# Weight combinations as sums of blocks made by adding transfers, and every second pair of blocks in turned order

## The chip, the cores and the metric

The kernel runs on one core of one Trainium2 chip. The metric is the device time of one execution in microseconds (us). Times inside an execution are counted from the start of the profiled span.

## The reference

Linear attention feeds a gated feed-forward block. Batch 4, 4 heads of 32 dims, sequence 1088, model width 128, feed-forward width 1024 (split in two halves of 512).

```python
kv = einsum('bhsf,bhsd->bhfd', phi(k), v);  z = sum_s phi(k)          # phi: product of two 8-dim sketches
x  = einsum('bhsf,bhfd->bhsd', phi(q), kv) / (phi(q) . z + 1e-6)       # -> [4, 1088, 128]
h  = gelu(x @ w_in);  u, v = h[..., :512], h[..., 512:]
v_n = (v - mean) / sqrt(var + 1e-6) * g_ln
v_s = einsum('ts,bsd->btd', w_sg, v_n) + b_sg[None, :, None]           # the large product, 1088 x 1088
out = x + (u * v_s) @ w_out
```

## The kernel before

**The large product.** `w_sg` (transposed, called `wd` in memory) is kept on chip in two words: `w_h`, the rounded one, and `w_l`, the rest. Every product of two values is made of three matmuls: high by high (L992), low by high (L993) and high by low (L994). The contraction over 1088 positions goes in nine tiles of 128 (the ninth has 64); `whole` runs all of them for one block of 128 features (`db`) and one third of the positions (`ci`, 362 to 364 columns). The ninth tile is added by `tail` (L1003, L1004).

**Seven products instead of eight.** Batches 1 to 3 treat two feature blocks at a time (`pair`), and of the nine tiles the first eight as two halves of four, and of the three column thirds the first two. That gives a 2x2 by 2x2 block product, which is made with seven block products (`product`, four tiles each) from combinations of the `v_n` blocks, made on VectorE (tile `tmp`, then `words` splits a combination into the buffer `ar`), and combinations of the weight blocks. The last column third goes through `whole` twice.

**Weight combinations.** `combine` makes them once. It loads pieces of `wd` into `tmp` (L1040, two transfers a step, eight steps), makes four combinations on VectorE (L1045 to L1048), splits each into two words (ScalarE L1050 to L1052, VectorE L1053 to L1055), and stores three of them, called "1", "3" and "2", to `td` in HBM (L1057 to L1059). The fourth stays on chip (`t4`). Plain block "b" is saved to `td` too. `stream(n, half)` later loads combination n into the middle third of `w_h` and `w_l`, over what lies there: two transfers of 362 KB (L1064) and four of 181 KB (L1066). It is called twice in batch 0 and four times in a pair, twice in the last pair.

**Attention of the next batch** (`attention(b)`) runs beside the pairs. Key features `kp` are made tile by tile: TensorE L1083, ScalarE L1086, VectorE L335, TensorE L1091. The query sketch goes out to `dq` in HBM (L1120) and comes back spread over the partitions as `ea` and `eb` (L1130, L1127), where VectorE multiplies them (L1133).

**Order.** A planner (`Plan`) writes the order of every engine before the program runs. The times that it aims at for TensorE's side work come from the tables `SIDE`, `UNITS` and `OUTS`. An engine executes its list in order, and so does the SyncE queue (SP) that issues nearly all transfers: an instruction that waits holds up all behind it.

## Time and profile before

| | |
|---|---|
| three runs | 346.93, 350.94, 351.39 us (median 350.94) |
| profiled execution | 347.09 us, of which the span is 345.3 us |
| busy | TensorE 332.4, VectorE 271.4, ScalarE 217.7, GpSimd 23.0 us |
| transfers | 68.87 MB, mean 199 GB/s |
| combination stores to `td` | 66.7 to 138.1 us of the span |

An engine's busy time says how much of the span it worked. TensorE's matmuls overlap, so its idle time is read between the starts of neighbouring matmuls: in an undisturbed stretch one of 362 columns starts 0.165 us after the one before.

### The profile page before, as it was taken

The numbers are of one execution on the slowest core, as the hardware profiler recorded it, in microseconds if no ns is written. First come the engines' busy times: TensorE is split into PE (matmuls) and PEld (weight loads), VectorE is DVE, ScalarE is ACT, GpSimd is POOL, SyncE is SP. The second block draws the span as 40 slices with busy tenths as digits, with TensorE's granted clock in tenths as the row PEclk, the third lists the DMA queues.
The fourth block names the chain that finished last, engine by engine and source line by source line (L and its number), as shares of the span: only waits on it lengthen the run. The fifth ranks groups of instructions, "written<-read, shape, count | busy, mean of one in ns | idle before, by whom it ended". The sixth has DMA issues, their size and how long they took to land.

```text
span 345.3 us, 5940 instructions
## 1 busy us (share of the span) xinstructions
PE 332.4 (96%) x1952; PEld 311.4 (90%) x1952; DVE 271.4 (79%) x619; ACT 217.7 (63%) x517; POOL 23.0 (7%) x86
## 2 busy tenths in 40 slices
PE   8998999999999979999999999999999999999995
PEld 7876559998999869889999999999999999999994
DVE  4798999998997598979973989989647765874764
ACT  5476862464579989637659986658979644332331
POOL 0002000000000330000002400000006000000000
PEclk9999999999999999999999999999999999999998
DMA  7996033566567755899996854784509905874601
GB/s 246 392 393 219 7 104 99 151 203 192 164 189 253 211 158 151 269 276 325 265 282 196 271 153 132 210 284 152 172 19 317 348 7 173 289 272 136 210 26 62
DMA packets 56175, 68.87 MB, mean 199 GB/s; under 512 B 5008, under 2 KB 53456, under 8 KB 56144
## 3 DMA queue, kind: packets, MB, share of 16 engines
q1 hardware_dynamic: 56000, 68.40, 63.2%
q8 instruction: 15, 0.25, 0.3%
q14 instruction: 16, 0.13, 0.1%
q10 hardware_dynamic: 144, 0.09, 0.1%
HBM read 59.48 MB, written 8.99 MB: 198 GB/s over the span
## 4 chain that ended last, share of the span: by engine, by line
PE 70%; DMA 13%; DVE 11%; issue 2%; ACT 2%; SPq 1%; DVEq 0%
PE bz L992 12%; PE bz L993 11%; PE bz L994 11%; DMA eb<-dq 4%; DMA td<-tmp 3%; PE pz L792 3%; PE bs L1091 2%; PE pab L668 2%; DMA tmp<-in_w 2%; DMA w_h<-td 2%; PE bs L906 2%; PE bs L907 2%; PE bs L908 2%; PE bz L1004 2%; PE bz L1003 2%
## 5 line engine op out<-in xcount | busy, mean ns | idle before, releaser
L992 PE MATMUL bz<-w_h,ar 128*128 128x362 f32 (+1 forms) x288 | 95.6, 332 | 1.9 <-DMA w_h<-td 1.3
L993 PE MATMUL bz<-w_h,ar 128*128 128x362 f32 (+1 forms) x288 | 94.7, 329 | 0.2 <-DVE ar L968 0.2
L994 PE MATMUL bz<-w_l,ar 128*128 128x362 f32 (+1 forms) x288 | 94.7, 329 | 0.0
L992 PEld LDWEIGHTS bz<-w_h,ar 128*128 128x128 f32 x288 | 54.3, 188 | 3.7 <-DMA w_h<-td 1.7
L993 PEld LDWEIGHTS bz<-w_h,ar 128*128 128x128 f32 x288 | 54.2, 188 | 1.0 <-DVE ar L968 0.5
L994 PEld LDWEIGHTS bz<-w_l,ar 128*128 128x128 f32 x288 | 54.2, 188 | 0.0
L967 ACT CAST ar<-vn 128x512 fp32r<-128x512 f32 x40 | 24.7, 620 | 23.1 <-PE bz L994 21.9
L936 ACT CAST gh<-gt 128x362 fp32r<-128x362 f32 (+1 forms) x47 | 23.1, 496 | 21.7 <-DVE gt L935 10.9
L968 DVE TENSOR_TENSOR ar<-vn,ar 128x512 fp32r<-128x512 f32 x40 | 27.3, 684 | 8.0 <-ACT ar L967 7.8
L912 ACT ACTIVATE u<-bs 128x362 f32<-128x362 f32 (+1 forms) x48 | 22.4, 470 | 15.4 <-PE bs L908 7.6
L937 DVE TENSOR_TENSOR gl<-gt,gh 128x362 fp32r<-128x362 f32 (+1 forms) x47 | 24.6, 532 | 6.7 <-ACT gh L936 6.6
L407 ACT ACTIVATE vn<-vn,st 128x512 f32<-128x512 f32 x36 | 27.7, 815 | 2.9 <-POOL st L538 2.3
L935 DVE TENSOR_TENSOR gt<-gt,u 128x362 f32<-128x362 f32 (+1 forms) x47 | 24.5, 529 | 1.5 <-ACT u L912 1.1
L922 DVE SCALAR_TENSOR_TENSOR gt<-bz,g_col,b_bc 128x362 f32<-128x362 f32 (+1 forms) x31 | 18.0, 588 | 6.4 <-PE bz L1004 4.1
L1188 ACT ACTIVATE kp<-vn,st 128x512 bf16<-128x512 f32 x27 | 19.5, 721 | 0.2
L1091 PE MATMUL bs<-vx,kp 128*128 128x128 f32 x108 | 16.4, 276 | 1.7 <-DVE kp L335 1.7
L792 PE MATMUL pz<-w_f,vn 128*128 128x362 f32 (+3 forms) x54 | 17.6, 472 | 0.3 <-ACT vn L407 0.3
L1185 ACT ACTIVATE vn<-bs 128x512 f32<-128x512 f32 x27 | 15.9, 590 | 1.7 <-PE bs L1178 1.7
L946 PE MATMUL po<-gl,wout_h 128*128 128x362 f32 (+1 forms) x47 | 15.7, 334 | 0.9 <-DVE gl L937 0.8
L1091 PEld LDWEIGHTS bs<-vx,kp 128*128 128x128 f32 x108 | 14.6, 191 | 2.0 <-DVE kp L335 2.0
L906 PE MATMUL bs<-x_h,win_h 128*128 128x362 f32 (+1 forms) x48 | 16.4, 341 | 0.0
L907 PE MATMUL bs<-x_h,win_l 128*128 128x362 f32 (+1 forms) x48 | 15.7, 328 | 0.0
(273 smaller groups left out, 744.7 us busy)
## 6 DMA issues: line engine op xcount, KB each, us to landing
w_l<-td SPq DMA_DIRECT2D x96, 181.0 KB, 5.0
w_h<-td SPq DMA_DIRECT2D x48, 362.0 KB, 4.4
w_f<-in_w SPq DMA_DIRECT2D x9, 544.0 KB, 11.2
tmp<-in_w SPq DMA_DIRECT2D x16, 181.0 KB, 2.8
vx<-in_v SPq DMA_DIRECT2D x8, 288.0 KB
ea<-dq SPq DMA_DIRECT2D x12, 182.0 KB, 3.1
eb<-dq SPq DMA_DIRECT2D x12, 182.0 KB
td<-tmp SPq DMA_DIRECT2D x8, 271.5 KB, 3.7
```

Of the source, the lines that this page charges most:

```text
L407: A.activation(self.vn(t), self.vn(t), AF.Identity, bias=self.nm[:, t : t + 1], scale=self.rs[:, t : t + 1])
L792: return mm(zs[ci], lhsT=vn[r, t, :P], rhs=w_f[t][r, c0 : c0 + cw], start=(t == 0), stop=(t == NT - 1),)
L906: mm(o, lhsT=win_h[:, ws], rhs=xh[:, cs], start=True, stop=False)
L935: add("V", dv(cw), lambda: V.tensor_mul(gt(k)[:, :cw], gt(k)[:, :cw], utt[plan.got[u]][:, :cw]), r=[u], w=[k], free=[u])
L936: add("A", ac(cw), lambda: A.copy(ght[plan.got[h]][:, :cw], gt(k)[:, :cw]), r=[k], take={h: "gh"})
L937: add("V", dv(cw), lambda: V.tensor_sub(glt[plan.got[l]][:, :cw], gt(k)[:, :cw], f32(ght[plan.got[h]][:, :cw])), r=[h, k], take={l: "gl"}, ...
L967: add("A", ac(n), lambda: A.copy(dst[:, 0], q()), r=r, w=[key])
L968: add("V", dv(n), lambda: V.tensor_sub(dst[:, 1], q(), f32(dst[:, 0])), r=r, w=[key])
L992: mm(o, lhsT=ar[e][:, 0, t], rhs=wh, start=first, stop=False, skip_group_check=True)
L993: mm(o, lhsT=ar[e][:, 1, t], rhs=wh, start=False, stop=False, skip_group_check=True)
L994: mm(o, lhsT=ar[e][:, 0, t], rhs=wl, start=False, stop=last, skip_group_check=True)
L1091: mm(ps(pkv)[:, P * p : P * p + P], lhsT=kpt[t % 3][:, P * p : P * p + P], rhs=vx[:, NT : NT + t + 2 : t + 1] if p else vx[:, t : NT + 1 : ...
```

## The change

The combinations become plain sums of blocks, so that they can be made outside the engines. `sums` copies a block of `wd` (or a finished sum) to a new HBM tensor `ud` (SyncE) and then lets GpSimd issue a transfer that adds a second block onto it. `combine` then only loads a sum, splits it into two words and stores them, through two buffers of `tmp` in turn. The signs that this moves go to the `v_n` combinations and to the gates (`g_col`, `ng_col`). Every first pair of a batch runs its seven products in turned order (`back`), so that it begins with the weight blocks that the pair before ended with. `stream` is now called once in batch 0 and twice in each pair. All tables of the planner are new, and `tmp` grows by one eighth, `rs` shrinks by a quarter.

```diff
-        k=[-69.5, -129.7, -258.62, 75.49, -16.81, -86.04, 99.22, -240.4, 467.74],
+        k=[-5.4506e+25, -1.86798e+26, -3.68831e+26, 1.20378e+26, -7.9147e+25, -9.67116e+25, 1.96766e+26, -2.06105e+26, 6.74955e+26],
...
-    rs = const([P, 4, P], "rs", F32R)
+    rs = const([P, 3, P], "rs", F32R)
-    tmp = const([P, 7 * HW], "tmp")
+    tmp = const([P, 8 * HW], "tmp")
...
+    ud = {n: dram.tile([P, 4, K2], F32, name=f"ud{n}") for n in "1324"}
+    def sums():
+        part = lambda i, j: wd[:, 4 * i : 4 * i + 4, K2 * j : K2 * j + K2]
+        for n, first, more in (("1", part(0, 0), part(0, 1)), ("2", "1", part(1, 1)), ("3", part(0, 1), part(1, 1)), ("4", "2", part(1, 0))):
+            u = isinstance(first, str)
+            load_("", 741, lambda n=n, f=first, u=u: load(ud[n], ud[f] if u else f), r=[("ud", first)] * u, w=[("ud", n)])
+            add("G", 1.2, lambda n=n, m=more: G.dma_start(ud[n], m, accum_op=ALU.add), w=[("ud", n)], late=7.0)
     def combine():
...
-                add("V", d, lambda s=s: V.tensor_sub(s[:, 0], s[:, 1], s[:, 0]), w=[k[0]], r=[k[1]])
-                add("V", d, lambda s=s: V.tensor_sub(s[:, 1], s[:, 3], s[:, 1]), w=[k[1]], r=[k[3]])
-                add("V", d, lambda s=s: V.tensor_sub(s[:, 3], s[:, 0], s[:, 3]), w=[k[3]], r=[k[0]])
-                add("V", d, lambda s=s, tl=tl: V.scalar_tensor_tensor(s[:, 2], s[:, 3], -1.0, s[:, 2], op0=ALU.mult, op1=ALU.subtract),
...
+        for i, (n, t) in enumerate((n, t) for n in "1234" for t in range(4)):
+            x, h = (tmp[:, 2 * K2 * (i % 2) + K2 * k :][:, :K2] for k in range(2))
+            load_("", 186, lambda n=n, t=t, x=x: load(x, ud[n][:, t]), r=[("ud", n)], w=[xk])
+            if n == "4":
+                add("A", ac(K2), lambda x=x, t=t: A.copy(t4(t)[0], x), r=[xk], w=[("t4", t)], after=[done_lo])
+                add("V", dv(K2), lambda x=x, t=t: V.tensor_sub(t4(t)[1], x, f32(t4(t)[0])), r=[xk], w=[("t4", t)])
+                continue
+            add("A", ac(K2), lambda x=x, h=h: A.copy(h, x), r=[xk], w=[hk])
+            add("V", dv(K2), lambda x=x, h=h: V.tensor_sub(f32r(x), x, f32(h)), r=[hk], w=[xk])
+            load_("td", 186, lambda n=n, t=t, h=h: load(TD[n][t, 0], f32(h)), r=[hk], w=[("td", n, t, 0)])
+            load_("td", 186, lambda n=n, t=t, x=x: load(TD[n][t, 1], x), r=[xk], w=[("td", n, t, 1)])
...
-    def pair(b, p, e, zi):
+    def pair(b, p, e, zi, back):
...
+        if back:
+            product(Z, zk, e[0], (0, 1), True, (1, 1))
+            stream("2", 0)
...
+            product(X, xk, e[1], (0, 0), True)
+            product(Z, zk, e[2], (4, 1), False, (1, 2))
+            stream("3", 4)
+            product(X, xk, e[3], (0, 1), False)
+            whole(Z, zk, 2, (e[1], e[0]), 0)
+            product(X, xk, e[2], (4, 1), False)
+            product(Z, zk, e[0], (4, 0), True, (0, 0))
+            product(X, xk, e[3], "t4", False, (0, 1))
+            whole(Z, zk, 2, (e[1], e[3]), 1)
+            return e[2], e[0], e[1], e[3]
...
         product(Z, zk, e[0], (0, 1), True, (1, 1))
-        if more:
-            stream("2", 0)
...
-        if more:
-            stream("3", 4)
...
+    sums()
...
         if ci == 1:
-            stream("2", 0)
-            stream("3", 4)
+            stream("1", 0)
...
-        pair(b, 0, e, zi)
+        e = pair(b, 0, e, zi, True)
...
-        pair(b, 1, e, 1 - zi)
+        e = pair(b, 1, e, 1 - zi, False)
```

On the SyncE queue, at the end of the loads of the head (the last `w_in` load is the first row), before the change `qld`, `vn` and `vx` (query, keys and values of batch 1) stand, and then the first pieces of `wd` for `combine`:

```order
L687 DMA win_raw_161<-in_w_in 128x512
L1108 DMA qld<-in_q 128x364
L1074 DMA vn<-in_k 128x9x128
L1073 DMA vx<-in_v 128x576 x2
L1040 DMA tmp<-in_w 128x2x181 x2
L1029 DMA td<-w_h 128x4x362
L1108 DMA qld<-in_q 128x364
```

And there now (`ud_610` is the sum "1", `ud_611` "3", `ud_612` "2"):

```order
L687 DMA win_raw_161<-in_w_in 128x512
L1034 DMA ud_610<-in_w 512x1x362
L1102 DMA qld<-in_q 128x364
L1068 DMA vn<-in_k 128x9x128
L1067 DMA vx<-in_v 128x576 x2
L1034 DMA ud_611<-in_w 512x1x362
L1038 DMA td<-w_h 128x4x362
L1044 DMA tmp<-ud_610 128x362 x2
L1102 DMA qld<-in_q 128x364
L1034 DMA ud_612<-ud_610 16x11584
```

One copy of a block moved ahead of the loads of batch 1, one behind them, and the loads of `tmp` now stand behind the store of `w_h` and wait for the first adding transfer.

On TensorE, at the end of the product of batch 0 over `w_f` (the weights as loaded), before the change the last four tiles run in one piece, and the first sketch of the keys of batch 1 follows:

```order
L792 MATMUL pz0_0_2_435<-w_f4_235,vn_91 128x364
L792 MATMUL pz0_0_0_431<-w_f5_243,vn_91 128x362
L792 MATMUL pz0_0_1_433<-w_f5_243,vn_91 128x362
```

Now six matmuls of later work stand between the fifth tile and the sixth:

```order
L792 MATMUL pz0_0_2_435<-w_f4_235,vn_91 128x364
L1077 MATMUL bs0_601<-sk_76,vn_91 128x128
L1108 MATMUL bs1_602<-qth_116,sk_h_78 128x364
L1109 MATMUL bs1_602<-qth_116,sk_l_79 128x364
L1110 MATMUL bs1_602<-qtl_117,sk_h_78 128x364
L1077 MATMUL bs2_603<-sk_76,vn_91 128x128
L1398 MATMUL bz0_604<-w_h_80,ar0_92 128x362
L792 MATMUL pz0_0_0_431<-w_f5_243,vn_91 128x362
```

Also on TensorE, at the key features of batch 2 (`kp`, and L1083 before, L1077 after, their sketch), before the change they follow each other with one small group between them:

```order
L946 MATMUL po0_2_890<-gl1_600,wout_h_86 128x364
L1091 MATMUL bs0_601<-vx_74,kp0_108 128x128 x2
L1083 MATMUL bs1_602<-sk_76,vn_91 128x128
L1091 MATMUL bs0_601<-vx_74,kp1_109 128x128 x2
L906 MATMUL bs2_603<-x0_h_153,win_h_84 128x364
L907 MATMUL bs2_603<-x0_h_153,win_l_85 128x364
L908 MATMUL bs2_603<-x0_l_154,win_h_84 128x364
L1091 MATMUL bs0_601<-vx_74,kp2_110 128x128 x2
L1083 MATMUL bs1_602<-sk_76,vn_91 128x128
L1091 MATMUL bs0_601<-vx_74,kp0_108 128x128 x2
```

Now the same features stand between the matmuls of a whole product:

```order
L994 MATMUL bz0_604<-w_l4_705,ar1_93 128x362
L1085 MATMUL bs0_601<-vx_74,kp2_110 128x128 x2
L1077 MATMUL bs2_603<-sk_76,vn_91 128x128
L1085 MATMUL bs0_601<-vx_74,kp0_108 128x128 x2
L992 MATMUL bz0_604<-w_h_80,ar1_93 128x362
L993 MATMUL bz0_604<-w_h_80,ar1_93 128x362
L994 MATMUL bz0_604<-w_l5_740,ar1_93 128x362
L1085 MATMUL bs0_601<-vx_74,kp1_109 128x128 x2
L906 MATMUL bs1_602<-x1_h_586,win_h_84 128x362
```

Large matmuls that TensorE did elsewhere now stand between the features, so that more time passes from one to the next.

More of the change, by code (lines that the diff above doesn't have):

```diff
@@ L1210, in pair @@
         a = {(i, j): area(b, 2 * p + i, j) for i in range(2) for j in range(3)}
         ak = {(i, j): vkeys(s, j, i) for i in range(2) for j in range(3)}
-        X, Z = (lambda: pzt[zi]), (lambda: pzt[1 - zi])
-        xk, zk = ("psn", zi), ("psn", 1 - zi)
+        banks = [(lambda: pzt[zi]), (lambda: pzt[1 - zi])]
+        bk = [("psn", zi), ("psn", 1 - zi)]
         c11, c12, c21, c22, ca, cb = (A1, 0), (A1, 1), (A2, 0), (A2, 1), (A1, 2), (A2, 2)
         end = b == B - 1 and p == 1
-        more = not end
@@ L1218, in both @@
-        def both(i, src, r):
-            add("A", ac(256), lambda: A.copy(rs[:, i : i + 2], src), r=r, w=[("rs", i), ("rs", i + 1)])
-            add("V", dv(256), lambda: V.tensor_sub(rs[64:, i : i + 2], src[64:], f32(rs[64:, i : i + 2])), r=r, w=[("rs", i), ("rs", i + 1)])
+        tk = [("tmp", i, k) for i in range(2) for k in range(2)]
+        def both(i, src, r, n):
+            w = [("rs", i + k) for k in range(n)]
+            add("A", ac(n * P), lambda: A.copy(rs[:, i : i + n], src), r=r, w=w)
+            add("V", dv(n * P), lambda: V.tensor_sub(rs[64:, i : i + n], src[64:], f32(rs[64:, i : i + n])), r=r, w=w)
@@ new lines, in rests, with total @@
+        def rests():
+            both(0, vn[:, 8, 256 * s : 256 * s + 256].rearrange("p (t d) -> p t d", d=P), ak[0, 2] + ak[1, 2], 2)
+            total(raw[:, 0], a[0, 2], a[1, 2], ak[0, 2] + ak[1, 2], ["raw"] + tk, V.tensor_sub, P)
+            both(2, raw, ["raw"], 1)
+        def total(out, x, y, r, w, f=V.tensor_add, n=512):
+            add("V", dv(n), lambda: f(out, x, y), r=r, w=w)
+        if back:
+            Z, X = banks
+            zk, xk = bk
+            total(sg, a[1, 0], a[1, 1], ak[1, 0] + ak[1, 1], ["sg"] + tk, V.tensor_sub)
+            words(ar[e[0]], lambda: sg, ("ar", e[0]), ["sg"])
+            split(b, A1, 0, e[1])
+            rests()
+            total(sg, sg, a[0, 0], ak[0, 0], ["sg"], V.tensor_sub)
+            total(s4, sg, a[0, 1], ["sg"] + ak[0, 1], ["s4"] + tk)
+            words(ar[e[2]], lambda: s4, ("ar", e[2]), ["s4"])
+            words(ar[e[3]], lambda: sg, ("ar", e[3]), ["sg"])
+            total(a[0, 0], a[0, 0], a[1, 0], ak[1, 0], ak[0, 0], V.tensor_sub)
+            product(Z, zk, e[0], (0, 1), True, (1, 1))
+            stream("2", 0)
+            split(b, A1, 1, e[0])
+            evac(b, c22, Z, zk, g_col)
+            unit(b, c12)
+            product(X, xk, e[1], (0, 0), True)
+            evac(b, c11, X, xk, g_col)
+            product(Z, zk, e[2], (4, 1), False, (1, 2))
+            stream("3", 4)
+            words(ar[e[2]], lambda: a[0, 0], ("ar", e[2]), ak[0, 0])
+            evac(b, c12, Z, zk, g_col)
+            unit(b, ca)
+            product(X, xk, e[3], (0, 1), False)
+            split(b, A2, 1, e[3])
+            evac(b, c12, X, xk, ng_col, ("gt", b, c12), False)
+            gate(b, c12)
+            unit(b, c22)
+            whole(Z, zk, 2, (e[1], e[0]), 0)
+            split(b, A2, 0, e[1])
+            evac(b, ca, Z, zk, g_col)
+            gate(b, ca)
+            unit(b, c11)
+            product(X, xk, e[2], (4, 1), False)
+            evac(b, c22, X, xk, ng_col, ("gt", b, c22), False)
+            gate(b, c22)
+            unit(b, c21)
+            product(Z, zk, e[0], (4, 0), True, (0, 0))
+            evac(b, c11, Z, zk, g_col, ("gt", b, c11), False)
+            gate(b, c11)
+            unit(b, cb)
+            product(X, xk, e[3], "t4", False, (0, 1))
+            evac(b, c21, X, xk, g_col)
+            gate(b, c21)
+            whole(Z, zk, 2, (e[1], e[3]), 1)
+            evac(b, cb, Z, zk, g_col)
+            gate(b, cb)
+            return e[2], e[0], e[1], e[3]
@@ L1222, in pair @@
+        X, Z = banks
+        xk, zk = bk
         split(b, A1, 0, e[0])
         split(b, A1, 1, e[1])
[L1224 to L1227 removed]
+        rests()
+        total(a[0, 0], a[0, 0], a[1, 0], ak[1, 0], ak[0, 0], V.tensor_sub)
@@ L1231, in pair @@
-        add("V", dv(P), lambda: V.tensor_scalar(raw[:, 0], a[1, 2], -1.0, None, op0=ALU.mult), r=ak[1, 2], w=rk)
-        add("V", dv(P), lambda: V.tensor_sub(raw[:, 1], raw[:, 0], a[0, 2]), r=ak[0, 2], w=rk)
-        both(2, raw, rk)
+        total(a[0, 1], a[0, 1], sg, ["sg"], ak[0, 1])
+        total(sg, a[1, 0], a[1, 1], ak[1, 0] + ak[1, 1], ["sg"], V.tensor_sub)
         unit(b, ca)
```

147 lines of the change are left out of this document (61 added, 86 removed).

## The prediction

> **What bounds the kernel now.** I read the page's first parts, then the engines' busy time by stretch, then TensorE's own order of time where it falls short.
>
> ```profile
> span 345.3 us, 5940 instructions
> PE 332.4 (96%) x1952; PEld 311.4 (90%) x1952; DVE 271.4 (79%) x619; ACT 217.7 (63%) x517; POOL 23.0 (7%) x86
> ...
> PE 70%; DMA 13%; DVE 11%; issue 2%; ACT 2%; SPq 1%; DVEq 0%
> ...
> 60.00:80.00 20.00, 20.00 (x128) 19.88 (x127) 17.89 (x36) 11.54 (x28) 1.01 (x1) 1.00 0.63 188
> 80.00:100.00 20.00, 19.17 (x111) 18.08 (x110) 18.90 (x46) 10.90 (x25) 0.00 (x0) 1.00 0.59 169
> 120.00:140.00 20.00, 17.29 (x115) 16.18 (x113) 18.10 (x47) 17.33 (x42) 3.21 (x11) 1.00 0.58 174
> 140.00:160.00 20.00, 18.55 (x108) 17.78 (x109) 17.02 (x36) 10.55 (x25) 0.00 (x0) 1.00 0.95 282
> 160.00:180.00 20.00, 20.00 (x120) 19.59 (x119) 17.03 (x33) 13.35 (x30) 0.00 (x0) 1.00 0.97 280
> 240.00:340.00 100.00, 100.00 (x594) 98.88 (x592) 66.41 (x132) 52.65 (x121) 6.37 (x22) 1.00 0.53 172
> ```
>
> The columns of the stretches are its length, then TensorE, weight loads, VectorE, ScalarE, GpSimd, the granted clock (1.00 throughout), the DMA share and GB/s. TensorE is busy in all of the last 100 us but for the tail, so nothing can be won there except by fewer matmuls. The DMA queues are at 0.95 to 0.97 from 140 to 180 us, and in the second half of that TensorE still loses nothing. TensorE falls short in 80 to 100 and 120 to 160 us, and there VectorE is at 17 to 19 of 20 us. So the question is which of a few stalls go. These are their rows (start, duration, what waited, and in brackets the idle time and what ended it):
>
> ```profile
> 43.40 7.78 PE L792 MATMUL pz<-w_f,vn 128*128 128x362 f32 x24 [0.31 <-ACT vn L407]
> ...
> 80.94 0.33 PE L945 MATMUL po<-gh,wout_l 128*128 128x362 f32 x1
> 81.64 0.43 PE L946 MATMUL po<-gl,wout_h 128*128 128x362 f32 x1 [0.37 <-DVE gl L937]
> 82.40 0.43 PE L992 MATMUL bz<-w_h,ar 128*128 128x362 f32 x1 [0.33 <-DVE gt L922]
> ...
> 120.19 0.32 PE L946 MATMUL po<-gl,wout_h 128*128 128x364 f32 x1
> 122.23 0.71 PE L1091 MATMUL bs<-vx,kp 128*128 128x128 f32 x4 [1.72 <-DVE kp L335]
> ...
> 125.22 0.49 PE L1083 MATMUL bs<-sk,vn 128*128 128x128 f32 x2
> 126.38 0.49 PE L1083 MATMUL bs<-sk,vn 128*128 128x128 f32 x2 [0.68 <-DVE kp L335]
> ...
> 139.94 0.43 PE L992 MATMUL bz<-w_h,ar 128*128 128x362 f32 x1 [0.29 <-DVE gt L922]
> ...
> 154.53 0.40 PE L1178 MATMUL bs<-win_l,x_h 128*128 128x512 f32 x1
> 156.19 0.43 PE L992 MATMUL bz<-w_h,ar 128*128 128x362 f32 x1 [1.26 <-DMA w_h<-td]
> ...
> 227.62 0.44 PE L946 MATMUL po<-gl,wout_h 128*128 128x362 f32 x1 [0.41 <-DVE gl L937]
> ```
>
> Each costs its bracket plus what the pipeline overlaps, which is start to start less the regular step of 0.17 us (0.23 for 512 columns): 0.70 - 0.17 and 0.76 - 0.17 at 81 and 82 us make 1.1; 2.04 - 0.17 = 1.9 at 120; 1.16 - 0.33 = 0.8 at 125; 1.66 - 0.23 = 1.4 at 154. For the other three I add 0.17 to the bracket: 0.5 at 43, 0.5 at 140, 0.6 at 227. The sum is **6.8 us**, and this is the ceiling of any gain: 2% of 347 us. Behind VectorE's lateness stand transfers:
>
> ```profile
> 80.22 0.92 DVE L1133 TENSOR_TENSOR ea<-ea,eb 128x728 f32<-128x728 f32 x1 [1.32 <-DMA eb<-dq]
> ...
> 120.93 0.92 DVE L1133 TENSOR_TENSOR ea<-ea,eb 128x728 f32<-128x728 f32 x1 [1.84 <-DMA eb<-dq]
> ...
> 141.45 0.69 DVE L1226 TENSOR_TENSOR tmp<-vn 128x512 f32<-128x512 f32 x1 [0.72 <-DMA td<-tmp]
> ...
> 225.76 0.91 DVE L1133 TENSOR_TENSOR ea<-ea,eb 128x720 f32<-128x720 f32 x1 [1.23 <-DMA w_l<-td]
> ```
>
> **The matmuls.** Both programs issue the same number of each kind (312 groups of the three large ones, 42 tails). So this term is zero, and the change can only move the stalls.
>
> **Fewer streams.** A stream is two transfers of 362 KB and four of 181 KB. The program before has 48 and 96 of them, as the rows say; the order of the new one has 26 and 52, so 13 streams for 24.
>
> ```profile
> w_l<-td SPq DMA_DIRECT2D x96, 181.0 KB, 5.0
> w_h<-td SPq DMA_DIRECT2D x48, 362.0 KB, 4.4
> ...
> tmp<-in_w SPq DMA_DIRECT2D x16, 181.0 KB, 2.8
> ```
>
> That takes out 11 x 1.45 = 16 MB of 68.9; the sums add four copies and four additions of 0.74 MB, some 6 to 9 MB. Where DMA is not waited for, this is worth nothing: at 160 to 180 us it is hidden by TensorE. What it is worth lies at 154 us. There the weights of the second product were issued as late as 148.94 and took 7.20 us in a full queue:
>
> ```profile
> 137.53 3.89 DMA td<-tmp
> ...
> 148.94 7.20 DMA w_h<-td
> ```
>
> They were late because the last store of a combination was issued at 137.5 and two streams could only then be finished. In the new program the one stream that the first pair begins with is of the sum "1", whose four stores are the first of twelve. I take the whole stall of **1.4 us** out; late next there is VectorE, whose lateness the row of 139.94 shows just before; I charge that below.
>
> **The combination on VectorE.** Seven lines of eight instructions go, 0.34 us each but for one of 0.52: these two rows stand for them.
>
> ```profile
> L1053 DVE TENSOR_TENSOR tmp<-tmp 128x362 fp32r<-128x362 f32 x8 | 4.2, 523 | 0.0
> ...
> L1045 DVE TENSOR_TENSOR tmp<-tmp 128x181 f32<-128x181 f32 x8 | 2.8, 345 | 1.5 <-DMA tmp<-in_w 1.5
> ```
>
> So 4.2 + 6 x 2.75 = 20.7 us before, and 16 of the first kind after, 16 x 0.523 = 8.4 us. 12 us less of VectorE in the stretch up to 138 us, in which it had little room. It counts only where VectorE's lateness reaches TensorE. At 120 us VectorE had itself waited 1.84 us on `eb`, so work taken away does not end that wait, but it does shorten the six features behind it; these now also stand among large matmuls, which gives each more time. I take half of 1.9 + 0.8: **1.4**. At 81 us likewise half of 1.1, **0.5**, since the same wait on `eb` stays in the program. At 140 us VectorE waited for a store out of `tmp`; the last users of `tmp` are now the four on-chip splits, which store nothing: **0.3** of 0.5. At 227 us less traffic, **0.3** of 0.6.
>
> **The six matmuls moved up.** They stand where TensorE idled at 43 us and wait for `vn`, `qld` and their casts. The last of those loads was out at 25.9 us (first row below); one copy of 0.74 MB is ahead of them now, and at the 280 GB/s of the full queue at 140 to 180 us that puts them 2.6 us later, still long before 42 us. I take **0.4** of 0.5.
>
> **The sums.** Nothing in the trace adds in HBM, so I bound it. GpSimd is free for it at 32.9 us, where its last small operation ends, and DMA then idles:
>
> ```profile
> 22.06 3.84 SPq L1073 DMA_DIRECT2D vx<-in_v  x2
> ...
> 42.09 0.37 SPq L1029 DMA_DIRECT2D td<-w_h  x1
> ...
> 32.74 0.20 POOL L538 TENSOR_TENSOR st<-np,st 128x3 f32<-128x3 f32 x1
> ...
> 30.00:40.00 10.00, 9.23 (x44) 6.53 (x43) 8.54 (x20) 6.47 (x13) 2.18 (x11) 1.00 0.15 48
> 40.00:50.00 10.00, 9.69 (x32) 5.58 (x31) 9.14 (x28) 8.54 (x17) 0.00 (x0) 1.00 0.30 94
> ...
> 52.50 0.18 ACT L1086 COPY kb<-bs 128x32 f32<-128x32 f32 x1
> ```
>
> The deadline is 52.5 us: the cast of the first sum stands behind that copy of `kb` on ScalarE, and behind it queue the next `kb` copies, on which TensorE's features wait at once. The load of the sum (2.8 us, row above) must be issued by 49.5; SyncE reaches it after the store of `w_h`, which went out at 42.1. So the first addition has from 33 to 49 us, **16 us**. Below: it costs what a plain transfer of its size does, two of 362 KB, 8.8 us, or less, since much of 4.4 us is latency. Above: two reads and a write, with the second addition beside it on the same engines, 4 x 8.8 = 35 us, and then TensorE loses 35 - 16 = 19 us. I take 9 us, the row it is nearest to, and so **nothing** for it on the path, hidden behind the preparation of the weights from 33 to 49 us. A gain below nothing is excluded: no one waits for it before.
>
> On what an addition costs, the Trainium skill, Collectives: The Full Stack, section "The bandwidth ceiling: the fold count and why AG ≠ RS ≠ AR", says that the adding step needs two source reads for each write and runs at half the rate of a copy. No trace of this kernel shows it yet; by it the addition is an estimated 17.6 us by the two 362 KB rows, 1.6 us over the deadline, and the sum would be 1.6 us smaller.
>
> **The sum.** 1.4 + 1.4 + 0.5 + 0.3 + 0.3 + 0.4 = 4.3 us. Against it, a new order on every engine brings waits of its own; the present one has seven, so I charge two of the small ones, 0.5 each. That leaves **-3.3 us**: 347.1 for the profiled execution becomes 343.8. The three runs shown lie at 346.9 and at 351 (median 350.94), where the same gain gives 347.6. I predict the middle of the two, **345.5 us**; the forecast's own range is 342 to 349.
>
> **The rivals.**
> *Nothing comes of it (20%).* For: `eb` comes by the same chain of SyncE steps, VectorE's 1.84 us stand before the features, and twelve casts of sums now stand in VectorE's and ScalarE's lists where each can hold up the rest. Against: the DMA-bound stall at 154 us has lost its cause. Time: 347.1 to 350.9, so 349.
> *All stalls go (15%).* For: all seven end in a transfer or in VectorE, and both get lighter. 347.1 - 6.8 = 340.3, or 344.1 by the median; 342.
> *The first addition comes late (12%), slower.* Mechanism: SyncE holds at the load of the first sum, then ScalarE at its cast, then TensorE at the key features. It decides from 49 us on, microsecond for microsecond. At 22 us for an addition (between the bounds of 8.8 and 35) it costs 6 and eats the gain; from there to 35 us it gives 350 to 363 us. For: SyncE's list is in order, and the query load for the next third stands behind it too. Against: 16 us of room and an idle DMA. The Trainium skill, SBUF — State Buffer, section "Who interferes with whom", says that VectorE in its two-port modes blocks GpSimd completely, the writing of its descriptors for transfers too, which would hold the addition back. The trace has a row on it:
>
> ```profile
> 68.89 1.01 POOL L805 MEMSET w_l<- 64x1088 f32 x1 [35.95 <-DVE w_l L806]
> ```
>
> GpSimd wrote 1088 columns in 1.01 us while VectorE was busy beside it with one subtraction of 1.28 us, so not every VectorE operation holds it up. VectorE's 8.5 of 10 us between 30 and 40 us are the most that could be lost, and that alone stays inside 16 us.
> *The change does not do what it says* has no room: the streams are counted in the order.
>
> **How the numbers follow.** Forecast 53%, rivals 20, 15 and 12%. Two per cent, 7 us, is about what a measurement of this kernel can tell from no change. Faster by more needs nearly the whole ceiling: the second rival and a little of the forecast, 0.16. Slower by more is most of the third, 0.09. Within 2%: 0.75. The range of 338 to 354 holds the forecast and the first two rivals with their scatter, and the mild half of the third.
>
> **What would show it.** Right: no wait on `w_h<-td` at the first pair of batch 1, 13 streams, DMA share well under 0.95 from 140 to 180 us, TensorE at 18.5 of 20 us or more from 120 to 140, and the first load of a sum issued right behind the store of `w_h`. Wrong: an idle SyncE before that load, ScalarE waiting at L1050, or TensorE waits of a kind not in the list above. I am wrong on size if the wait of VectorE on `eb` goes or doubles.

## The result, and the profile after

The changed kernel takes 359.23 us (median of 4 runs, 356.97 to 360.87), the one before 349.39 us (median of 4 as well). The ratio is 1.0316, with a 95% interval of 1.0264 to 1.0368: it is **slower by 3.2%**. The forecast was 345.5 us in a range of 338 to 354. The profiled execution took 360.87 us, with a span of 359.1 us, 13.8 us longer than before. Ratios, here and below, are taken over the fast runs alone, while the medians of the table further down count every run (one of e11 took 548 us, one of e13 843).

The first lines of the page, the engines' shares of the chain of waits, and the issues of the streams:

```profile
span 359.1 us, 5751 instructions
PE 338.1 (94%) x1952; PEld 316.2 (88%) x1952; DVE 260.0 (72%) x573; ACT 214.1 (60%) x509; POOL 28.4 (8%) x90
...
PE 58%; DMA 16%; ACT 10%; DVE 8%; SPq 2%; issue 2%; POOL 1%; POOLq 0%; DVEq 0%; ACTq 0%
...
w_l<-td SPq DMA_DIRECT2D x52, 181.0 KB
w_h<-td SPq DMA_DIRECT2D x26, 362.0 KB
```

There are as many matmuls as before (x1952), VectorE has 11.4 us less to do (271.4 before), and 13 streams are left of 24. All this came as planned. But TensorE's part of the chain fell from 70% to 58%. The stretches say where (columns as in the prediction; the seventh number is the granted clock, the eighth the DMA share):

```profile
60.00:80.00 20.00, 16.97 (x101) 16.58 (x100) 14.36 (x25) 8.03 (x21) 2.20 (x2) 0.91 0.92 248
80.00:100.00 20.00, 12.65 (x61) 12.21 (x60) 11.03 (x23) 6.41 (x14) 0.00 (x0) 0.76 0.70 163
120.00:140.00 20.00, 17.97 (x108) 17.14 (x107) 9.58 (x24) 16.11 (x45) 5.04 (x22) 0.91 0.60 176
140.00:160.00 20.00, 19.85 (x121) 19.14 (x120) 17.82 (x35) 12.95 (x29) 0.00 (x0) 1.00 0.73 223
160.00:180.00 20.00, 20.00 (x123) 19.99 (x122) 19.71 (x43) 12.13 (x25) 0.00 (x0) 1.00 0.33 105
```

From 140 to 180 us the relief is there: the DMA share is 0.73 and 0.33, where it was 0.95 and 0.97, and TensorE is short of 0.15 us where it was short of 1.45. The loss lies ahead of that, from 60 to 100 us, where TensorE lost nothing and 0.8 us before and loses 3.0 and 7.4 us now. TensorE's own order of time has the three stalls:

```profile
68.56 0.60 PE L1396 MATMUL bz<-w_l,ar 128*128 128x362 f32 x2 [3.03 <-DVE w_l L806]
...
94.51 0.67 PE L906 MATMUL bs<-x_h,win_h 128*128 128x362 f32 x1 [7.35 <-ACT u L912]
...
133.71 0.71 PE L1085 MATMUL bs<-vx,kp 128*128 128x128 f32 x4 [2.03 <-DVE kp L335]
```

and VectorE's, just ahead of each, has one instruction that waits for the same transfer each time:

```profile
66.38 0.92 DVE L1127 TENSOR_TENSOR ea<-ea,eb 128x728 f32<-128x728 f32 x1 [4.20 <-DMA eb<-dq]
...
92.16 0.92 DVE L1127 TENSOR_TENSOR ea<-ea,eb 128x728 f32<-128x728 f32 x1 [8.35 <-DMA eb<-dq]
...
132.41 0.92 DVE L1127 TENSOR_TENSOR ea<-ea,eb 128x728 f32<-128x728 f32 x1 [2.61 <-DMA eb<-dq]
```

VectorE works in order, so the low words of the weights (first stall) and the key features (third) stand behind that multiplication. In the second stall TensorE waits for `u`, and ScalarE's order of time shows that `eb` was not the only late transfer there:

```profile
89.08 0.49 ACT L1103 CAST qth<-qld 128x364 fp32r<-128x364 f32 x1 [8.21 <-DMA qld<-in_q]
...
92.89 0.49 ACT L1050 CAST tmp<-tmp 128x362 fp32r<-128x362 f32 x1 [2.39 <-DMA tmp<-ud]
93.29 0.79 ACT L1128 CAST r<-ea 128x728 fp32r<-128x728 f32 x1
93.99 0.46 ACT L912 ACTIVATE u<-bs 128x364 f32<-128x364 f32 x1
```

ScalarE waited for the query load, then for the load of a finished sum, which landed at 92.9 us, later than `eb` at 92.2; `u` stands behind that cast and behind the cast of the product `ea` (L1128), which could have begun at 93.1. So, by these rows, `eb` alone on time would have shortened this stall little. The list of waits puts the waits on `eb` at 20.2 us, against 5.5 before. Beside `eb` on the DMA engines, at 57 to 66 and at 82 to 92 us, are the third and fourth additions to go out (of sums 2 and 4; the order is 1, 3, 2, 4). GpSimd's order of time has their issues, and the view of their line the time until they landed:

```profile
33.16 1.48 POOL L1035 DMA_DIRECT2D ud<-in_w  x1
44.45 1.21 POOL L1035 DMA_DIRECT2D ud<-in_w  x1 [9.66 <-issue]
56.76 1.16 POOL L1035 DMA_DIRECT2D ud<-in_w  x1 [11.11 <-issue]
77.23 1.19 POOL L1035 DMA_DIRECT2D ud<-in_w  x1 [5.96 <-DMA ud<-ud]
```

```profile
DMA to landing us min/median/max: 10.8/11.5/13.6
```

The DMA part of the page, taken for 59.5 to 66 us and for 80 to 85 us, shows how the additions (q0, GpSimd's queue) and everything that SyncE issues (q1) share the 16 engines. The columns are packets, MB, and the time of the packets as a share of the engines' time:

```profile
q0 software_dynamic: 508, 0.72, 75.7%
q1 hardware_dynamic: 449, 0.60, 29.9%
...
q0 software_dynamic: 412, 0.59, 89.4%
q1 hardware_dynamic: 169, 0.23, 19.1%
```

The engines are full (the two shares overlap and come to over 100%), and SyncE's queue gets 30% and 19% of them: 0.60 MB in 6.5 us is 92 KB a microsecond, 0.23 MB in 5 us is 46. Before, from 160 to 180 us, the same queue moved 280. So `eb`, 364 KB that SyncE had issued by 58.4 us, landed at 66.4, and the one that it issued from 81.9 on at 92.2. The third stall is another matter: it has no addition beside it, as the fourth had landed by 90.8 us, and the kernel before had 1.72 us in that place.

A second loss rides on the stalls. Behind each of them the granted clock is low (stretches behind the first and the second):

```profile
70.00:74.00 4.00, 4.00 (x17) 4.00 (x17) 3.23 (x6) 2.03 (x5) 1.01 (x1) 0.60 0.98 270
...
94.00:102.00 8.00, 7.49 (x29) 7.50 (x30) 6.58 (x15) 4.80 (x13) 0.00 (x0) 0.59 0.53 164
```

TensorE is busy there, but at 0.60 and 0.59 of its clock, which loses 0.40 x 4.0 + 0.41 x 7.5 = 4.7 us of work. Before, the clock was 1.00 in every stretch shown. The page's first lines split the 13.8 us: TensorE idles 21.0 us where it idled 12.9, which is 8.1 more, and the same matmuls keep it busy for 338.1 us instead of 332.4, which is 5.7 more. The three stalls, 12.4 us against 6.8 in all seven before, are most of the first part. The slow clock behind the first two stalls is most of the second, and more of it lies behind the third (0.91 from 120 to 140 us).

### The profile page after: what moved, and what is told of

Read it like the earlier page. It is cut to its first block, busy times and chain, and to the rows that moved or that the text cites. A ratio compares the mean times of both kernels' runs of the same rounds, so it can differ in the third digit from the quotient of the medians.

```text
span 359.1 us, 5751 instructions
## 1 busy us (share of the span) xinstructions
PE 338.1 (94%) x1952; PEld 316.2 (88%) x1952; DVE 260.0 (72%) x573; ACT 214.1 (60%) x509; POOL 28.4 (8%) x90
## 3 DMA queue, kind: packets, MB, share of 16 engines
q0 software_dynamic: 2112, 2.97, 6.2%
## 4 chain that ended last, share of the span: by engine, by line
PE 58%; DMA 16%; ACT 10%; DVE 8%; SPq 2%; issue 2%; POOL 1%; POOLq 0%; DVEq 0%; ACTq 0%
PE bz L992 10%; PE bz L994 10%; PE bz L993 10%; DMA eb<-dq 8%; DMA tmp<-ud 3%; DMA td<-tmp 3%; PE pz L792 3%; ACT vn L407 2%; PE pab L668 2%; ACT kp L1182 2%; DMA dq<-ab 2%; PE bs L1085 2%; ACT vn L1179 2%; PE bs L906 2%; PE bs L908 1%
## 5 line engine op out<-in xcount | busy, mean ns | idle before, releaser
L992 PE MATMUL bz<-w_h,ar 128*128 128x362 f32 (+1 forms) x288 | 97.3, 338 | 0.7 <-ACT ar L967 0.3
L993 PE MATMUL bz<-w_h,ar 128*128 128x362 f32 (+1 forms) x288 | 95.4, 331 | 0.0
L992 PEld LDWEIGHTS bz<-w_h,ar 128*128 128x128 f32 x288 | 55.0, 191 | 2.9 <-DVE gt L922 1.7
L993 PEld LDWEIGHTS bz<-w_h,ar 128*128 128x128 f32 x288 | 55.0, 191 | 0.5
L994 PEld LDWEIGHTS bz<-w_l,ar 128*128 128x128 f32 x288 | 55.0, 191 | 0.0
L912 ACT ACTIVATE u<-bs 128x362 f32<-128x362 f32 (+1 forms) x48 | 22.6, 472 | 20.1 <-PE bs L908 13.6
L967 ACT CAST ar<-vn 128x512 fp32r<-128x512 f32 x37 | 22.8, 618 | 16.9 <-PE bz L994 15.9
L922 DVE SCALAR_TENSOR_TENSOR gt<-bz,g_col,b_bc 128x362 f32<-128x362 f32 (+1 forms) x37 | 21.9, 592 | 10.3 <-PE bz L1004 8.0
L968 DVE TENSOR_TENSOR ar<-vn,ar 128x512 fp32r<-128x512 f32 x37 | 25.3, 686 | 5.6 <-ACT ar L967 5.4
L906 PE MATMUL bs<-x_h,win_h 128*128 128x362 f32 (+1 forms) x48 | 17.0, 355 | 7.4 <-ACT u L912 7.4
L1127 DVE TENSOR_TENSOR ea<-ea,eb 128x728 f32<-128x728 f32 (+1 forms) x9 | 8.2, 914 | 20.2 <-DMA eb<-dq 20.2
L906 PEld LDWEIGHTS bs<-x_h,win_h 128*128 128x128 f32 x48 | 9.4, 196 | 8.2 <-ACT u L912 7.7
```

The lines of the kernel that those rows point to most:

```text
L906: mm(o, lhsT=win_h[:, ws], rhs=xh[:, cs], start=True, stop=False)
L968: add("V", dv(n), lambda: V.tensor_sub(dst[:, 1], q(), f32(dst[:, 0])), r=r, w=[key])
L992: mm(o, lhsT=ar[e][:, 0, t], rhs=wh, start=first, stop=False, skip_group_check=True)
L993: mm(o, lhsT=ar[e][:, 1, t], rhs=wh, start=False, stop=False, skip_group_check=True)
L994: mm(o, lhsT=ar[e][:, 0, t], rhs=wl, start=False, stop=last, skip_group_check=True)
```

## The experiments

**Theory A** was that the additions occupy the DMA engines, slow what is moved beside them, `eb` above all, and that TensorE's stalls follow from there through VectorE's list. **Rival B** was that the new order of the lists makes things late, whatever is moved. Unless told otherwise a kernel keeps every instruction in its place.

| run | us | ratio to before (95%) |
|---|---|---|
| changed kernel | 359.23 | 1.0316 (1.0264 to 1.0368) |
| e1: additions of 16 bytes a row | 350.02 | 1.0005 (0.9966 to 1.0044) |
| e2: copies in place of additions | 354.51 | 1.0164 (1.0114 to 1.0215) |
| e3: before, and the sums beside it | 372.89 | 1.0691 (1.0635 to 1.0747) |
| e4: turned order, sums on VectorE | 357.52 | 1.0223 (1.0151 to 1.0296) |
| e5: second and fourth addition small | 349.56 | 1.0011 (0.9964 to 1.0058) |
| e6: additions and copies small | 347.87 | 0.9987 (0.9949 to 1.0026) |
| e7: turned order, sums on GpSimd | 367.13 | 1.0526 (1.0457 to 1.0595) |
| e8: additions planned with 13 us | 360.41 | 1.0325 (1.0258 to 1.0392) |
| e9: second addition small | 356.02 | 1.0187 (1.0109 to 1.0266) |
| e10: fourth addition small | 353.77 | 1.0142 (1.0081 to 1.0203) |
| e11: sums 3 and 4 on VectorE | 349.21 | 1.0009 (0.9977 to 1.0041) |
| e12: e3 with small additions | 357.87 | 1.0202 (1.0115 to 1.0289) |
| e13: e6, `ea` and `eb` not from `dq` | 347.46 | 0.9939 (0.9897 to 0.9981) |
| e14: before, the same | 349.66 | 0.9982 (0.9934 to 1.0030) |
| e15: e13, two loads behind `eb` | 348.49 | 0.9974 (0.9932 to 1.0016) |
| e16: e6, two loads behind `eb` | 352.66 | 1.0051 (1.0011 to 1.0091) |
| e17: third addition small | 355.99 | 1.0210 (1.0107 to 1.0314) |
| e18: third and fourth addition small | 350.79 | 1.0024 (0.9981 to 1.0067) |

Prices are differences of ratios, times 349.5 us; by the intervals of the two ratios each is uncertain by 2 to 4 us. The additions are counted in the order in which they go out.

### What the additions cost

```diff
-            add("G", 1.2, lambda n=n, m=more: G.dma_start(ud[n], m, accum_op=ALU.add), w=[("ud", n)], late=7.0)
+            add("G", 1.2, lambda n=n, m=more: G.dma_start(ud[n][:, :, :4], m[:, :, :4], accum_op=ALU.add), w=[("ud", n)], late=7.0)
```

> The changed kernel with every instruction in its place, but each addition moves 16 bytes of every row instead of 1448 (the sums then lack most of their second block). Theory A (the additions occupy the DMA engines and slow whatever is moved beside them; from there eb is late, VectorE's list holds, TensorE stalls): the waits of VectorE on eb fall from 20 us to under 8, the stalls of 3.2 us at 65 and 7.5 us at 87 go, and the time falls from 359 to 344 to 349. Rival B (the new order of the lists makes eb late, whatever is moved): the stalls at 65 and 87 stay, 355 to 360.

The time is that of before, 1 us above theory A's range and far below rival B's, so the bytes of the four additions are all of the loss: 1.0316 - 1.0005 is 10.9 us, give or take 2.3. VectorE waits 8.8 us for `eb`. SyncE's queue had the engines nearly to itself while `eb` was on its way, at 57 to 60 us and at 76 to 82:

```profile
q1 hardware_dynamic: 412, 0.55, 58.9%
...
q1 hardware_dynamic: 720, 0.94, 78.2%
```

That is 183 and 157 KB a microsecond where it had been 92 and 46. The stall at 65 us is gone. Of that at 87 us 2.3 us are left, ahead of 85.4 us, which the bytes of the additions don't explain. Theory A holds, rival B doesn't.

In e2 the four transfers move the same bytes without adding.

```diff
-G.dma_start(ud[n], m, accum_op=ALU.add)
+G.dma_start(ud[n], m)
```

> The changed kernel, but the four GpSimd transfers copy the second block over the first instead of adding it (same bytes, rows and issues; the sums then lack their first block). Theory A1 (it is the adding: 135 ns for a row of 1448 bytes where a copied one takes 62): a transfer lands in 5 to 7 us instead of 11.5, most of the stalls at 65 and 87 go, 345 to 350. Rival A2 (any 0.74 MB on GpSimd's queue in that stretch does it): it lands in 9 us or more, 354 to 360. Rival B (the order alone): 355 to 360 though it lands early.

By its numbers rival A2 has it, at the lower edge: 354.5 us, and 9.7 us to landing at the median (7.3 to 10.4). But the time is half way, so half of the loss (5.6 us) is there for a plain copy too, and the other half (5.3 us) comes with the adding. The pages show what each costs the DMA engines. The first two lines are of the changed kernel, the third of this one:

```profile
q1 hardware_dynamic: 39680, 55.05, 48.9%
q0 software_dynamic: 2112, 2.97, 6.2%
```

```profile
q0 software_dynamic: 768, 2.97, 4.1%
```

6.2% of 16 x 359.1 us over 2112 packets is 169 ns for 1406 bytes, 120 ns a KB. The copy within HBM takes 4.1% of 16 x 352.6 us over 768 packets, 301 ns for 3867 bytes, 78 ns a KB. SyncE's ordinary transfers take 71 ns for 1387 bytes, 51 ns a KB. My 62 ns for a copied row was the price of SyncE's ordinary transfers, the wrong kind of copy. Adding costs 1.5 times a copy within HBM, and 2.4 times what the transfers beside it cost. The copy also went in longer packets (2 or 3 rows to one), so this run doesn't tell the adding from the shorter packets that come with it.

The next five take the additions apart: some of them move 16 bytes of a row, the others all. The first edit stands for all, with other names of sums in its list.

```diff
-G.dma_start(ud[n], m, accum_op=ALU.add)
+G.dma_start(*((x if n in "12" else x[:, :, :4]) for x in (ud[n], m)), accum_op=ALU.add)
```

> The changed kernel, every instruction in its place, with the third and fourth additions (sums 3 and 4) moving 16 bytes of a row and the first two whole (sums 3 and 4 then lack most of a block). Theory A (an addition costs by what it lies beside: the third went out at 56.8 us with eb of the first third, the fourth at 77.2 with eb of the second): both large stalls go, 350 to 352. Rival D (the first two delay the whole list: the second could only go out at 44.5, and everything behind stands 6 to 7 us later from 80 us on): 355 to 359.

> The changed kernel, every instruction in its place, only the third addition (issued at 56.8 us there) with 16 bytes of a row (sum 3 then lacks most of a block). Theory A, with shares by the stalls of the changed kernel: the stall of 3.2 us at 65 us and the slow clock behind it go (4 to 5 us), and what stands behind comes earlier; the one at 87 us stays at 4 to 8 us: 353 to 357. Rival: the fourth follows the third in every list, so all of it goes, 349 to 351.

> The same with only the fourth addition small (issued at 77.2 us). Theory A: the stall at 65 us stays at 3 us, that at 87 us shrinks from 7.5 to about the 2.5 us that it has with all additions small: 352 to 356. Rival: the late list behind the third addition alone makes the stall at 87, 357 to 360.

The first two of these expectations took sum 3 for the third to go out, and it is the second: e5 has the second and fourth small, e9 the second. So their numbers don't bear on the theories as written, and two more runs were made.

> The expectations of e5, e9 and e10 named the additions by their sums; the order in which they go out is sums 1, 3, 2, 4. So e5 had the second and fourth out small, e9 the second, e10 the fourth, and the third out was whole in all three. Here only the third out (sum 2, at 56.8 us in the changed kernel) is small, the second whole. Theory A (an addition costs by the transfers that lie beside it): nothing lies beside the first eb at 57 to 66 us, so the stall of 3.2 us at 65 us is under 1, the fourth still costs its 6 us: 354 to 357. Rival G (the second is the one that costs, since the load of sum 1 and what stands behind it lie beside it): the stall at 65 us stays over 2 us, 358 to 361.

> The changed kernel with the last two that go out (sums 2 and 4) small and the first two (sums 1 and 3) whole: what e5 was meant to be. Theory A: all of the loss goes, 348 to 351. Rival G (the second to go out costs what e9 saved, 4.5 us): 353 to 356.

e18 is even with the kernel before: the first two additions, whole, cost nothing that can be measured, and the last two all of it, 10.2 us. The third alone costs 3.7 us (e17), the fourth 6.1 (e10), together 9.8. By its time alone e17's price, 3.7 give or take 4.0 us, is not clear of nothing; what shows it is that the stall of 3.03 us is gone. Theory A holds, rival G falls. The stalls agree. TensorE's and VectorE's waits of e17, with the third out of the way, and of e10, with the fourth:

```profile
DVE ea L1127 <- DMA eb<-dq: 13.5, 5, 8.0
...
PE bs L906 <- ACT u L912: 6.8, 1, 6.8
```

```profile
DVE ea L1127 <- DMA eb<-dq: 13.6, 7, 6.1
...
PE bz L1396 <- DVE w_l L806: 5.0, 1, 5.0
```

In each the stall of the other addition stays; in e10 it is 5.0 us instead of 3.0. And e9 is no contradiction. The second addition costs 4.5 us there though it lies beside nothing that waits, since it decides when the third goes out (GpSimd's order of time in e9):

```profile
46.19 1.21 POOL L1035 DMA_DIRECT2D ud<-in_w  x1 [10.67 <-issue]
54.31 1.16 POOL L1035 DMA_DIRECT2D ud<-in_w  x1 [6.91 <-DMA ud<-ud]
```

With a small second one the third, whole, goes out at 54.31 us instead of 56.76, and the stall at 65 us is 1.19 us instead of 3.03. As e9 still has the 6.1 us of the fourth, little of its 6.4 us over e1 is left for the third: the same 0.74 MB cost some 4 us or next to nothing by 2.5 us of place, as far as these intervals tell.

e8 changes one number of the planner, so its lists differ.

```diff
-w=[("ud", n)], late=7.0)
+w=[("ud", n)], late=13.0)
```

> The changed kernel with one number of the planner changed: an addition is taken to land 13 us after its issue instead of 7 (it took 10.8 to 13.6). So casts and loads of the sums stand later in every list. Theory A (other transfers are slowed, eb above all): eb is still late, 353 to 360. Rival C (the lists wait in order on sums that were planned for too early): 345 to 350.

360.4 us: lists that give the additions 13 us gain nothing, and rival C falls. Theory A's range is missed by 0.4 us only, but its wait was wrong. The third and fourth addition went out at 63.6 and 90.5 us, `eb` was waited for 6.8 us in all, and ScalarE waited for the load of a finished sum:

```profile
79.17 0.49 ACT L1050 CAST tmp<-tmp 128x362 fp32r<-128x362 f32 x1 [4.45 <-DMA tmp<-ud]
...
104.95 0.49 ACT L1050 CAST tmp<-tmp 128x362 fp32r<-128x362 f32 x1 [4.14 <-DMA tmp<-ud]
```

TensorE stalled 4.2 us at 76 us and 3.5 at 103. Whatever transfer lies beside or behind the addition and is next in a list pays for it.

e3 puts the copies and additions into the kernel before, with nobody reading the sums; e12 is the same with additions of 16 bytes.

```diff
+    sums()
     unit(0, (1, 0))
```

> The kernel before with the four copies and four additions of the new one put into its program; nobody reads the sums, so the streams, the pairs and the combination on VectorE are those of before. Theory A: the additions slow the transfers beside them here too, VectorE's waits on eb grow from 5.5 us to over 12, and the time rises by 5 to 14 us, to 355 to 363. Rival B (the order of the new lists): no one waits for the sums, so 348 to 351.

> Control for the kernel before with the sums (372.9): the same lists, with additions of 16 bytes of a row. Theory A: additions are nearly all of the 23 us, 348 to 353. Rival B (the four copies, or the lists that were planned anew around them): 360 or more.

The additions alone raise the time by 4.9%, 17 us, without any turned order: more than I expected, as all four ran beside the key features there (52.7 to 97 us; TensorE stalled 8.2 and 6.3 us on `kp`). But e12 is at neither number: 7 us, give or take 3, are left for four copies of 0.74 MB and the lists planned around them. So e3 is not clean as a price, though it shows theory A's mechanism in another program.

e6 makes the copies small too, and loads plain blocks.

```diff
-load(ud[n], ud[f] if u else f)
+load(ud[n][:, :, :4], (ud[f] if u else f)[:, :, :4])
...
-load(x, ud[n][:, t])
+load(x, wd[:, t, :K2])
```

> The changed kernel's lists with nothing of weight moved within HBM: copies and additions move 16 bytes of a row, and the loads of the sums read a plain block of the weights in their place (the sums are then plain blocks). It prices the four copies, against the run with small additions at 350.0. Theory A (the 2.3 us packets of 46 KB of the second and fourth copy, and two more copies in the full queue before 33 us, cost something beside eb too): 346 to 349, the stall of 2.5 us at 83 smaller. Rival B (that stall comes from the order): 350, with the stall at 83 still there.

347.9 us. The copies are worth 0.2% against e1, within the intervals. The stall at 83 us fell from 2.33 to 1.08 us in the one profile of each.

### Where the expected gain was

e6 is the order of the changed kernel with nothing in its way, and it is no faster than before. So the 4.3 us that the prediction credited did not come: the interval leaves room for a gain of 1.8. Its stalls (TensorE's order of time):

```profile
83.74 0.43 PE L906 MATMUL bs<-x_h,win_h 128*128 128x362 f32 x1 [1.08 <-ACT u L912]
...
93.00 0.50 PE L1170 MATMUL bs<-win_h,x_h 128*128 128x512 f32 x1 [1.53 <-ACT r L1143]
...
121.63 1.23 PE L1085 MATMUL bs<-vx,kp 128*128 128x128 f32 x4 [2.56 <-DVE kp L335]
```

The one on the key features was 1.72 us before. VectorE was quite idle ahead of it; it waited 2.51 us for `eb` at 120.33 us.

e13 takes `ea` and `eb` from an input, so that they need not wait for `dq` to land; e14 does so in the kernel before.

```diff
-load(o[:, p], dq[ci][32 + 16 * p : 48 + 16 * p, :cw].unsqueeze(0).broadcast_to([R, 16, cw]))
+load(o[:, p], qd[b, 32 + 16 * p : 48 + 16 * p, cs].unsqueeze(0).broadcast_to([R, 16, cw]))
```

> The order alone (347.9 us, copies and additions of 16 bytes), and ea and eb loaded from the query sketch's input instead of from dq: same bytes, same places in every list, but their issue no longer waits for the store to dq to land (what is multiplied then isn't the sketch). In that run the stall of 2.7 us at 119 us followed a chain: dq stored at 108.5, landed 4.6 us later, ea and eb issued by 116, eb landed 4.8 us later. Theory E (the chain of three transfers sets this stall, so VectorE's 11 us less could not shorten it): the wait of VectorE on eb and the stall go, with the slow clock behind it, 343 to 346. Rival (VectorE's and ScalarE's lists set it): the stall stays over 2 us, 347 to 349.

> The same edit in the kernel before, where I had given half of the stalls of 1.9 and 0.8 us at 120 and 125 us and of 1.1 at 81 to VectorE's lateness. Theory E: these go almost whole without any work taken from VectorE, 344 to 347 beside some 349. Rival: they stay, 348 to 350.

Theory E fell, and the time is the rival's. e13 is 0.6% below before, and its stall on `kp` is still 2.4 us; e14 is even with before, with a stall of 1.3 us on `kp`. In e13 SyncE reached `ea` no sooner: the next instruction of its list, a load into `tmp`, went out at 114.34 us, after a store out of `tmp` that had been issued at 109.20.

e15 moves that load and one other behind `eb`, in e13; e16 does it in e6.

> The run before this one without the wait on dq (347.5 us, stall of 2.6 us at 120.7 still there), with two loads of sums moved behind eb in SyncE's list, the one right ahead of ea at 114.3 us among them. Theory F (SyncE's list was held by that load, which waits until a store out of the same half of tmp has landed, as long as dq takes to land; either alone holds ea and eb): SyncE reaches ea at 112, VectorE's wait on eb and the stall fall under 1 us, 343 to 346. Rival (VectorE's and ScalarE's lists): the stall stays over 2 us, 347 to 349.

> The same two loads moved behind eb, but ea and eb loaded from dq as in the order alone (347.9 us). Theory F: the landing of dq still holds ea, so the stall stays at 2 to 3 us and the time at 347 to 349. Rival (the load of the sum alone holds SyncE): the stall goes, 343 to 346.

In e15 SyncE reaches `ea` at 112.53 us, and VectorE's waits on `eb` are 1.6 us in all, against 5.3 in e13. The stall stays, and the time is the rival's: the cast of the sum is now the one that waits, for the load that stands behind (ScalarE's order of time; the lines of these two kernels are 14 higher):

```profile
120.58 0.49 ACT L1064 CAST tmp<-tmp 128x362 fp32r<-128x362 f32 x1 [2.81 <-DMA tmp<-in_w]
```

TensorE waits 1.93 us for `kp` at 122.38. In e16, with `dq` still waited for, the same chain makes 4.0 us, and the time, 352.7 us, lies above both expectations. So theory F is right on what held SyncE, and wrong on what would come of it. Three transfers of about equal lateness (`dq` to `eb`, the store out of `tmp`, the load of the next sum) feed one place in the lists, and whichever goes, the next is there. None of these five runs is faster than before by 2%.

### The parts apart

e4 has the turned order and 13 streams, with the sums made on VectorE in the eight steps of before (`V.tensor_add` in place, no `ud`); e7 the same with the sums on GpSimd. Their lists are planned anew.

```diff
-add("V", d, lambda s=s: V.tensor_add(s[:, 0], s[:, 0], s[:, 1]), w=[k[0]], r=[k[1]])
+add("G", 0.5, lambda s=s: G.tensor_add(s[:, 0], s[:, 0], s[:, 1]), w=[k[0]], r=[k[1]])
```

> The other part of the change alone: the turned order of every second pair and 13 streams for 24, with the tables of the new program, but the sums made on VectorE in the eight steps of before (two loads of 362 KB from the weights, four additions in place, splits, three stores), so no copies and no additions within HBM. Theory A: the turned order and fewer streams are worth what I had counted for the stall at 154 us (1.4 us) and no more than 3 us in all, 344 to 350. Rival B (the turned order is what costs): 354 to 362.

> The turned order with sums made on the chip as in the run without additions in HBM (357.5), but the four sums of a step by GpSimd instead of VectorE, so VectorE's share is that of the changed kernel and nothing is moved within HBM. If VectorE's 11 us of sums are what made that run slow (its stall of 2.8 us at 141 us stood behind VectorE and ScalarE), 346 to 351. If it was the order of the lists, 354 to 358. If GpSimd and VectorE slow each other, VectorE's mean times rise and it is over 356.

e4 has the number of rival B, 2.2% slower than before (1.5 to 3.0), and its longest stall is of the turned pair itself. The pair now begins with a combination of `v_n` blocks (VectorE L1228), its cast and its rest, before its first product, and VectorE was busy for 10.5 of the 12 us up to 142:

```profile
144.40 0.43 PE L992 MATMUL bz<-w_h,ar 128*128 128x362 f32 x1 [2.64 <-ACT ar L967]
```

So the turned order has a price when VectorE makes the sums too, which e6 doesn't show. But e4 also has the changed kernel's tables, made for a lighter VectorE, and lists of its own, so how much of the 2.2% is the order and how much is the tables stays open.

In e7 GpSimd takes 0.58 to 0.80 us where VectorE takes 0.34 for the same piece, and its first sums wait for loads:

```profile
L1048 POOL TENSOR_TENSOR tmp<-tmp 128x181 f32<-128x181 f32 x8 | 6.4, 797 | 0.6
...
L1045 POOL TENSOR_TENSOR tmp<-tmp 128x181 f32<-128x181 f32 x8 | 4.7, 584 | 52.9 <-DMA tmp<-in_w 52.9
```

VectorE's splits behind them took 0.34 us for 181 columns, as in e4, and 0.58 instead of 0.52 for 362, so the two hardly slow each other; why the run is 10 us over e4 was not taken apart.

e11 is a whole kernel: sums 1 and 2 by additions within HBM, sums 3 and 4 on VectorE just ahead of the cast.

```diff
+        load(x, wd[:, t, K2 : 2 * K2] if n == "3" else ud["2"][:, t])
+        load(h, wd[:, t + 4, K2 : 2 * K2] if n == "3" else wd[:, t + 4, :K2])
...
-A.copy(h, x)
+(n == "3" and V.tensor_add(x, x, f32(h)), A.copy(h, x))
```

> A whole kernel: sums 1 and 2 by additions within HBM as in the changed one, sums 3 and 4 by VectorE, which adds a second loaded block just ahead of the cast (eight more additions of 128 x 362, eight more loads, and the third and fourth copy and addition gone); all else in the place that it has in the changed kernel. Theory A: as with two additions small (349.6) plus some of 4 us of VectorE and of eight loads, 349 to 353. Rival (VectorE's work in that stretch costs as in the run with all sums on VectorE, 357.5): 355 or more.

349.2 us: it regains the loss and is even with the kernel before. Eight sums on VectorE and eight more loads cost nothing that can be measured. No version ran faster than before by 2%.

## Why the prediction was wrong

**The step that failed** is the one headed "The sums": "I take 9 us, the row it is nearest to, and so **nothing** for it on the path". It priced one addition, the first, against one deadline, the cast of the first sum. There it was nearly right. The first addition took 11.0 us, its load went out at 44.20 us, well ahead of the 49.5 us that I had worked out, and e18 shows that the first two cost nothing. But there are four, and I asked only who waits for a sum, never who is beside it on the engines. The third and fourth, at 57 and 77 us, lie beside `eb`, which the prediction had itself quoted with waits of 1.32 and 1.84 us, and beside the loads that ScalarE waits for, and cost 3.7 and 6.1 us where the prediction had nothing. The bound of 35 us for an addition came from plain transfers, and was no bound for its neighbours.

**The rival of the same sign** had another mechanism: SyncE holding at the first load, from 22 us for an addition on. That did not happen; additions took 10.8 to 13.6 us. Its 12% were on the right side for the wrong reason. On the size of an addition the Trainium skill, Collectives: The Full Stack, "The bandwidth ceiling: the fold count and why AG ≠ RS ≠ AR", had half the rate of a copy; e2 makes it 1.5 times the time of a copy within HBM, whose packets were longer. Of the sharing, the Trainium skill, DMA: Bandwidth & Descriptors, "Queues, rings and completion order", says that each engine takes turns between the queues packet by packet. In the first stretch above the 508 packets to 449 agree with it, the 412 to 169 of the second don't, and why is open. By that rule a queue with dear packets takes the larger share of time, as the 76% to 30% and 89% to 19% show.

**The streams** were right in what they do (26 and 52 transfers, no wait on `w_h<-td` at the first pair, DMA share 0.73 and 0.33), and that stall of 1.4 us is gone. **VectorE's relief** was right in size (11.4 us for my 12), and wrong in worth: half of the stalls at 81, 120 and 125 us was credited to it. The stall at 120 grew to 2.56 us in e6 with VectorE idle ahead of it; e13, e15 and e16 show three transfers that feed it, one behind another. The prediction had the row with `eb` and took half all the same. The row that it set behind the stall at 139.94 us, VectorE's wait of 0.72 us, ends at 141.45, after that stall, so it can't have been its cause. **The matmuls** as a zero term were right by count, but the turned pair has a longer way to its first product, which e4 prices at a stall of 2.6 us when VectorE is loaded; I charged nothing for it by name. **The six matmuls moved up** were credited with 0.4 us, and TensorE still waits 0.51 us for `vn` at 43.87. **The charge of 1.0 us** for new waits had no room for the additions. From the forecast of -3.3 us to the measured ratio are 4.1%, 14.3 us: 10.9 are the additions (e1), and the other 3.4 are the gain that did not come.

**Of the signs** set out beforehand those for the streams came true; the first load of a sum right behind the store of `w_h`, and TensorE from 120 to 140 us (17.97 us for 18.5), missed. All the signs for wrong came: SyncE idle ahead of the first load of a sum (2.5 us, up to 44.20), ScalarE waiting at L1050 (5.2 us in all), TensorE waits of new kinds (L1396 on `w_l`, L906 on `u`), and the wait on `eb`, which grew from 5.5 to 20.2 us.

## What to carry to other kernels

A transfer in the background has two prices: when its own result is needed, and what it does to every transfer beside it. The second is looked up for each of its occurrences: what is in flight there, and which engine has an instruction that waits for it at the head of a list in order. And where a wait is fed by several transfers of equal lateness, nothing is credited for removing one until the row of the next has been found.
